# Early partial sums stored straight into the result, late ones added to it by accumulating transfers

## The chip, the cores and the metric

The kernel runs on one core of one Trainium2 chip. The metric is the device time of one execution in microseconds. A profiled execution gives a trace beside it, whose span runs from the first to the last instruction.

## What is computed

An attention through 32 memories for each of 8 heads, over 8 sequences of 576 tokens, followed by a two-layer network with a squared ReLU on all 4608 tokens. Cut to what matters here:

```
a   = softmax(phi)                          # over the 32 memories
k_m = einsum('bhsm,bhsd->bhmd', a, k);  v_m = einsum('bhsm,bhsd->bhmd', a, v)
x   = softmax(q @ k_m.T / 8) @ v_m          # heads side by side: 4608 x 512
h   = relu(x @ w_in)                        # 4608 x 2048
out = (h * h) @ w_out                       # 4608 x 512, float32
```

The kernel keeps the result transposed, as `outT` (512 x 4608) in HBM.

## The kernel before

A float32 product is made of three TensorE products of rounded halves (`x_hi`, `x_lo` and likewise for the weights). The first two sequences (`FUSED = 2`) go through both layers at once. For the other six (3456 tokens) the first layer writes its output to HBM (`r_f32`), and `second_layer` (from L1231) runs at the end, when everything else is done.

`second_layer` goes through a list of items (L1235 to L1237). An item is a stretch of tokens and `p`, one of eight pairs of blocks of 128 rows of `w_out`. Six stretches of 512 tokens are done by `products` (L1339), with a scheme that makes seven products out of eight; the 384 tokens that are left (`rest`) are done by `plain` (L1322), with ordinary products. These 384 tokens stand in the list twice: with `p` from 0 to 5 (`EARLY = 6`) ahead of all the stretches, and with `p` 6 and 7, the last quarter, behind all of them. So each of the four blocks of 128 output rows (`e` from 0 to 3, `NET = 4`) has two partial sums, some 240 us apart:

- Ahead (L1466 to L1468): when `p` is 5, ScalarE copies the four PSUM banks to SBUF rooms named `m23` and `sums`, and SyncE (SP, an engine that only issues transfers) stores them to a scratch tensor `part_f32` in HBM.
- Behind: after the last stretch SP loads the scratch tensor into the tile `part` (named `y`), L1475. Then the last `plain` items run, and `outputs` (L1407) makes five steps: VectorE adds a bank of PSUM to its part of the tile (L1412), and the sum is stored to `outT` (L1416). Block 3 goes in two halves of 192 tokens; SP issues the first four stores and ScalarE's queue the last one.

Just ahead of `outputs` on VectorE stand the sums of the last stretch (`finish_up`, L1386, whose adds and stores are recorded under L1356 and L1350).

The order on each engine is as written (a manual schedule); the tile framework sets the waits on semaphores. A transfer's semaphore is one of eight lanes, shown as `DMAHW0` to `DMAHW7`.

Of the kernel before, what the change touches and what calls it, by code (L numbers as in the profile page):

```python
# [13 lines left out]
ALU = mybir.AluOpType  # L14
# [10 lines left out]
def attn_moe_kernel(ctx: ExitStack, tc: tile.TileContext, qT, kv, phi, w_in, w_out, outT):  # L25
# [12 lines left out]
    nc = tc.nc  # L38
    ctx.enter_context(tc.manual_schedule())

    B, NQ, S = kv.shape[:3]
    P = 128
# [19 lines left out]
    FUSED = 2  # L62
# [1140 lines left out]
    for k, step in enumerate(steps):  # L1203
        i, f = step
        pieces = runs[i][0]
        n = f * P // FC
# [9 lines left out]
        g, rest = ffn1(f, parts, T, k, "act" if k in SQ_ACT else "dve", k < WHOLE and f in whole)  # L1216
# [14 lines left out]
    def second_layer():  # L1231

        late = (B - FUSED) * S
        rest = late % (2 * HALF)
# [6 lines left out]
        def load(i, room=None):  # L1241
            if i < len(items):
                t0, n, p = items[i]
                raw[i] = sp.tile([P, 4 * HALF], F32, name=room)[:, :2 * n] if room else xp.tile([P, 2 * n], F32, name="raw")
                nc.sync.dma_start(
                    out=raw[i].rearrange("p (a n) -> p a n", a=2), in_=r_f32[p][:, :, t0:t0 + n]
                )

        def square(i):
            if i < len(items):  # L1250
                n = items[i][1]
                y[i] = xp.tile([P, 2 * n if n == rest else 8 * HALF], F32, name="y", bufs=3)
                nc.scalar.activation(y[i][:, :2 * n], raw.pop(i), AF.Square)  # L1253
# [11 lines left out]
        def high(i):  # L1265
            if i < len(items):
                if items[i][1] != rest:
                    y[i] = y[i][:, HALF:]
                x[i] = [xp.tile([P, y[i].shape[-1]], F32R, name=n) for n in ("x_hi", "x_lo")]
                nc.scalar.copy(x[i][0], y[i])  # L1270
# [23 lines left out]
        def fetch_w(p):  # L1294
            if p < NFT // 2:
                w_of[p] = sp.tile([P, 2, DM], F32, name=("m01", "m45")[p % 2])
                nc.sync.dma_start(out=w_of[p], in_=w_out_f32[p])

        def weights(p):

            w = w_of.pop(p)
            half = DM // 2
            v = sp.tile([P, 4, half], F32, name=("m23", "sums")[p % 2])
            combine_w(w, v)
            W[p] = rooms_w(p) if p < 5 else [sp.tile([P, 4, half], F32R, name=f"s_{n}{p}") for n in ("hi", "lo")]
            yield
            nc.scalar.copy(W[p][0], v)
            yield
            nc.vector.tensor_tensor(out=W[p][1], in0=v, in1=W[p][0].bitcast(F32), op=ALU.subtract)

        def plain(i, acc):

            _, n, p = items[i]
            todo = [(2 * p + k, e) for k in range(2) for e in range(NET)]
            if p >= EARLY:
                todo = [(2 * p + k, e) for e in range(NET - 1) for k in range(2)]
            if p == NFT // 2 - 1:
                todo += [(f, NET - 1) for f in range(2 * EARLY, NFT)]
            for f, e in todo:
                y = x[i + f // 2 - p]  # L1320
                for j, (v, u) in enumerate(((0, 0), (1, 0), (0, 1))):
                    nc.tensor.matmul(  # L1322
                        acc[e][:, :n], wo[f][:, v, e * P:(e + 1) * P], y[u][:, f % 2 * n:(f % 2 + 1) * n],
                        start=f in (0, 2 * EARLY) and j == 0, stop=f in (2 * EARLY - 1, NFT - 1) and j == 2,
                    )

        def products(i, acc):

            p = items[i][2]
            f0, f1 = wo[2 * p], wo[2 * p + 1]  # L1330
            for m, of, col, z in (
                (0, f0, 0, 0), (1, W[p], 2, 5), (2, W[p], 1, 4), (3, W[p], 0, 3),
                (4, f1, 0, 2), (5, f1, DM // 2, 6), (6, W[p], 3, 1),
            ):
                for e in range(2):
                    for j, (v, u) in enumerate(((0, 0), (1, 0), (0, 1))):
                        at = col + e * P
                        w = of[v][:, col, e * P:(e + 1) * P] if of is W[p] else of[:, v, at:at + P]
                        nc.tensor.matmul(  # L1339
                            acc[m][:, e * HALF:(e + 1) * HALF], w, x[i][u][:, z * HALF:(z + 1) * HALF],  # L1340
                            start=p == 0 and e == 0 and j == 0, stop=p == NFT // 2 - 1 and e == 1 and j == 2,
                        )
# [43 lines left out]
        def finish_up(acc, t0):  # L1386

            m = rooms_m()
            nc.scalar.copy(m[0], acc[0])
            add(m[1], acc[1], m[0])  # L1390
            add(m[2], acc[2], m[1])
            nc.scalar.copy(m[3], acc[3])
            yield
            add(m[1], m[1], m[3])
            add(m[4], acc[4], m[0])
            store(t0, 0, 1, m[4])
            add(m[3], m[3], m[2])
            store(t0, 1, 0, m[3])
            add(m[5], acc[5], m[2])
            store(t0, 1, 1, m[5])  # L1400
            add(m[6], acc[6], m[1])
            store(t0, 0, 0, m[6])

        part_f32 = dram.tile([P, NET, rest], F32, name="part_f32")
        part = end = None

        def outputs(acc):  # L1407

            cols = [(e, 0, rest) for e in range(NET - 1)]
            cols += [(NET - 1, 0, rest // 2), (NET - 1, rest // 2, rest)]  # L1410
            for e, c0, c1 in cols:
                nc.vector.tensor_tensor(  # L1412
                    out=part[:, e, c0:c1], in0=acc[e][:, c0:c1], in1=part[:, e, c0:c1], op=ALU.add
                )
                nc_q = nc.scalar if c0 else nc.sync
                nc_q.dma_start(  # L1416
                    out=outT[e * P:(e + 1) * P, FUSED * S + c0:FUSED * S + c1], in_=part[:, e, c0:c1]
                )

        load(4, "s_hi6")  # L1420
# [8 lines left out]
        for i, (t0, n, p) in enumerate(items):  # L1429
            first, last = p == 0, p == NFT // 2 - 1  # L1430
            if n == rest:
                if p in (0, EARLY):
                    names = ("b0", "b1", "b2", "b3") if first else ("b3", "b4", "b7", "b5")
                    acc = [ps.tile([P, 512], F32, name=x) for x in names]
                plain(i, acc)
            else:
                if first:
                    acc = [ps.tile([P, 512], F32, name=f"b{(4 + m) % 8}") for m in range(7)]
                products(i, acc)
            if i >= 4:  # L1440
                load(i + 4)
            high(i + 1)
            square(i + 3)
            if due:
                next(due)
            if rest_of:
                rest_of()
                rest_of = None
            for fn, k in ((low, 1), (combine, 2)) if n == rest else ((combine, 2), (low, 1)):
                fn(i + k)  # L1450
            if end:
                next(end, None)
                end = None
            new = None
            if i in PLACES:
                new = weights(PLACES[i])
                next(new)
                fetch_w(PLACES[i] + 2)
            if due:
                next(due, None)  # L1460
            due = new
            if sum_up and next(sum_up, True):
                sum_up = None
            if n == rest and p == EARLY - 1:
                o = [sp.tile([P, 2, 2 * HALF], F32, name=x) for x in ("m23", "sums")]
                for e in range(NET):  # L1466
                    nc.scalar.copy(o[e // 2][:, e % 2, :n], acc[e][:, :n])
                    nc.sync.dma_start(out=part_f32[:, e], in_=o[e // 2][:, e % 2, :n])  # L1468
            elif last and n == rest:
                outputs(acc)  # L1470
            elif last and t0 + n == late:
                end = finish_up(acc, t0)
                next(end)
                part = xp.tile([P, NET, rest], F32, name="y", bufs=3)
                nc.sync.dma_start(out=part, in_=part_f32)  # L1475
            elif last:
                rest_of, sum_up = take_apart(acc, t0)

# [101 lines left out]
```

## Time and profile before

| | |
|---|---|
| time, median of 3 runs | 693.61 us (693.13 to 695.61) |
| the profiled execution's own time | 693.01 us |
| its span | 690.9 us |
| TensorE busy with products | 680.3 us (98%) |
| VectorE / ScalarE / GpSimd (POOL) busy | 75% / 58% / 9% |
| granted TensorE clock over the span | 0.999 of full speed |

TensorE is busy nearly all the time, so what another engine does counts only where TensorE waits for it, or after TensorE's last product. In the page's names, PE is TensorE, DVE is VectorE, ACT is ScalarE, POOL is GpSimd, SPq and ACTq are the queues of SyncE and ScalarE that issue transfers. A transfer's row has the duration of its issue; its landing is counted from the start of that issue.

### The profile page before, as it was taken

Reading aid. Unit: us, or ns where it says so; the run is one execution under the profiler, and the core shown is the slowest. Engines: PE = TensorE matmul, PEld = TensorE weight load, DVE = VectorE, ACT = ScalarE, POOL = GpSimd, SP = SyncE. Lnnn points to the kernel's source line nnn. Section 1 sums busy time; section 2 is a strip of 40 time slices with the busy share of each in tenths; the row PEclk is TensorE's granted clock in tenths of the full one; section 3 lists DMA queues with packets and bytes.
Section 4 is the critical chain, followed back from the end, with each engine's and each line's share of the span. In section 5 each row is a group of like instructions: output and inputs, shape, how many; then the busy total and the mean of one; then the engine's idle time right before and its main releaser. Section 6 shows DMA issues by size and latency. Waiting matters only on the chain.

```text
span 690.9 us, 14437 instructions
## 1 busy us (share of the span) xinstructions
PE 680.3 (98%) x5860; PEld 614.1 (89%) x5860; DVE 517.6 (75%) x888; ACT 401.6 (58%) x620; POOL 60.9 (9%) x86
## 2 busy tenths in 40 slices
PE   9899999999999999999999999999999999999998
PEld 5477798988889878888888899999999999999997
DVE  4978787987666847585847635998979798897964
ACT  2647887975554555555555565766555555555541
POOL 1322102101321010101000000000000000000000
PEclk9999999999999999999999999999999999999999
DMA  9993528263693969595946579643444536344434
GB/s 302 391 345 111 216 88 261 65 226 118 205 353 129 298 212 327 194 329 189 347 154 215 190 239 330 200 120 93 152 124 122 153 93 183 100 146 128 130 95 153
DMA packets 95218, 135.16 MB, mean 196 GB/s; under 512 B 5616, under 2 KB 60144, under 8 KB 94512
## 3 DMA queue, kind: packets, MB, share of 16 engines
q1 hardware_dynamic: 92192, 129.09, 57.0%
q10 hardware_dynamic: 2960, 5.15, 2.1%
q8 instruction: 46, 0.75, 0.5%
q14 instruction: 20, 0.16, 0.1%
HBM read 87.29 MB, written 46.92 MB: 194 GB/s over the span
## 4 chain that ended last, share of the span: by engine, by line
PE 82%; DMA 9%; ACT 5%; DVE 2%; SPq 1%; issue 1%; POOL 0%; ACTq 0%; DVEq 0%
PE b L1339 35%; PE hh L1500 13%; PE acc L748 11%; PE h L697 7%; DMA r_f<-o 7%; PE b L1322 5%; PE ps_m L430 4%; PE acc L740 3%; ACT o L1531 2%; PE h L310 2%; DMA wo<-in_w_in 1%; DMA u_hi<-in_kv 1%; ACT u_hi L577 1%; PE h L168 1%; ACT e_sb L266 1%; PE h L430 1%
## 5 line engine op out<-in xcount | busy, mean ns | idle before, releaser
L1270 ACT CAST x_hi<-y 128x1792 fp32r<-128x1792 f32 (+1 forms) x56 | 87.9, 1570 | 104.2 <-PE b L1339 50.5
L1274 DVE TENSOR_TENSOR x_lo<-y,x_hi 128x1792 fp32r<-128x1792 f32 (+1 forms) x56 | 104.7, 1870 | 44.7 <-ACT x_hi L1270 44.7
L1531 ACT ACTIVATE o<-hh 128x576 f32<-128x576 f32 x94 | 61.2, 657 | 83.4 <-PE hh L1500 52.2
L1339 PE MATMUL b<-x_hi,wo 128*128 128x256 f32 x576 | 107.8, 283 | 0.0
L1339 PEld LDWEIGHTS b<-x_hi,wo 128*128 128x128 f32 x576 | 89.9, 192 | 0.0
L1339 PE MATMUL b<-x_lo,wo 128*128 128x256 f32 x288 | 81.4, 283 | 0.0
L1263 DVE TENSOR_TENSOR y<-y 128x512 f32<-128x512 f32 x144 | 73.6, 512 | 3.3
L1339 PE MATMUL b<-x_lo,u_hi 128*128 128x256 f32 x240 | 67.5, 281 | 0.0
L1339 PE MATMUL b<-x_hi,u_hi 128*128 128x256 f32 x240 | 67.4, 281 | 0.0
L1339 PE MATMUL b<-x_hi,u_lo 128*128 128x256 f32 x240 | 67.4, 281 | 0.0
L1253 ACT ACTIVATE y<-raw 128x1024 f32<-128x1024 f32 (+1 forms) x52 | 53.6, 1031 | 4.7 <-DMA raw<-r_f 4.7
L1339 PEld LDWEIGHTS b<-x_lo,wo 128*128 128x128 f32 x288 | 55.3, 192 | 0.0
L1339 PEld LDWEIGHTS b<-x_hi,u_hi 128*128 128x128 f32 x240 | 46.0, 192 | 0.0
L1339 PEld LDWEIGHTS b<-x_lo,u_hi 128*128 128x128 f32 x240 | 45.1, 188 | 0.0
L1339 PEld LDWEIGHTS b<-x_hi,u_lo 128*128 128x128 f32 x240 | 45.0, 188 | 0.0
L748 PE MATMUL acc<-g_hi,wo 128*128 128x320 f32 (+1 forms) x256 | 43.2, 301 | 0.0
L1339 PE MATMUL b<-x_lo,s_hi 128*128 128x256 f32 x144 | 40.5, 282 | 0.0
L1339 PE MATMUL b<-x_hi,s_hi 128*128 128x256 f32 x144 | 40.5, 281 | 0.0
L1339 PE MATMUL b<-x_hi,s_lo 128*128 128x256 f32 x144 | 40.5, 281 | 0.0
L705 ACT ACTIVATE r_room<-h 128x320 f32<-128x320 f32 (+2 forms) x56 | 24.7, 442 | 26.7 <-PE h L697 25.9
L748 PEld LDWEIGHTS acc<-g_hi,wo 128*128 128x128 f32 x256 | 38.0, 188 | 0.8 <-ACT wo L677 0.8
L740 PE MATMUL acc<-g_hi,wo 128*128 128x256 f32 (+1 forms) x128 | 34.1, 409 | 0.0
(269 smaller groups left out, 1633.6 us busy)
## 6 DMA issues: line engine op xcount, KB each, us to landing
r_f<-o SPq DMA_DIRECT2D x48, 576.0 KB, 4.3
raw<-r_f SPq DMA_DIRECT2D x46, 512.0 KB, 4.0
wo<-in_w_in SPq DMA_DIRECT2D x16, 512.0 KB, 8.2
wo<-in_w_out SPq DMA_DIRECT2D x16, 512.0 KB, 7.0
kvb<-in_kv SPq DMA_DIRECT2D x28, 256.0 KB, 6.1
q_sb<-in_q SPq DMA_DIRECT2D x24, 288.0 KB, 5.3
out_t<-m SPq DMA_DIRECT2D x24, 256.0 KB, 2.3
e_sb<-in_phi SPq DMA_DIRECT2D x8, 512.0 KB, 4.2
```

Source lines behind the costliest of these rows:

```text
L430: nc.tensor.matmul(out[half][M * pr:M * (pr + 1), :y.shape[-1]], mem[hs, x, pr], y, start=True, stop=True)
L697: nc.tensor.matmul(h[:, at:at + n], u[:, qd, fs], x[:, qd], start=(i == 0), stop=(i == len(todo) - 1))
L740: nc.tensor.matmul(acc[e][:, :T], wo[f][:, e * P:(e + 1) * P], g_hi, start=first, stop=last)
L748: nc.tensor.matmul(acc[e][:, :T], wo[f][:, w, e * P:(e + 1) * P], x, start=first and x is g_hi and w == 0, stop=last and x is g_lo,)
L1253: nc.scalar.activation(y[i][:, :2 * n], raw.pop(i), AF.Square)
L1263: nc.vector.tensor_tensor(out=out, in0=in0, in1=in1, op=ALU.subtract)
L1270: nc.scalar.copy(x[i][0], y[i])
L1274: nc.vector.tensor_tensor(out=x[i][1], in0=y.pop(i), in1=x[i][0].bitcast(F32), op=ALU.subtract)
L1322: nc.tensor.matmul(acc[e][:, :n], wo[f][:, v, e * P:(e + 1) * P], y[u][:, f % 2 * n:(f % 2 + 1) * n], start=f in (0, 2 * EARLY) and j == 0 ...
L1339: nc.tensor.matmul(acc[m][:, e * HALF:(e + 1) * HALF], w, x[i][u][:, z * HALF:(z + 1) * HALF], start=p == 0 and e == 0 and j == 0, stop=p ...
L1500: nc.tensor.matmul(banks[t][:, :T], u[:, qd, fs], x[:, qd], start=(i == 0), stop=(i == len(todo) - 1))
L1531: nc.scalar.activation(r.rearrange("p (t x) -> p t x", t=NT), h[:, :, :S // NT], AF.Relu)
```

## The change

The early partial sums are stored into `outT` itself in place of the scratch tensor, by the same four transfers from SP. The load of the scratch tensor is gone. At the end VectorE no longer adds; it copies the late partial sums from PSUM to the tile, and five transfers that GpSimd issues add them to what stands in `outT` (`accum_op=ALU.add`). No transfer of `outputs` is left on SP or on ScalarE's queue.

```
-                nc.vector.tensor_tensor(
-                    out=part[:, e, c0:c1], in0=acc[e][:, c0:c1], in1=part[:, e, c0:c1], op=ALU.add
-                )
-                nc_q = nc.scalar if c0 else nc.sync
-                nc_q.dma_start(
-                    out=outT[e * P:(e + 1) * P, FUSED * S + c0:FUSED * S + c1], in_=part[:, e, c0:c1]
+                nc.vector.tensor_copy(part[:, e, c0:c1], acc[e][:, c0:c1])
+                nc.gpsimd.dma_start(
+                    out=outT[e * P:(e + 1) * P, FUSED * S + c0:FUSED * S + c1], in_=part[:, e, c0:c1], accum_op=ALU.add
                 )
...
-                    nc.sync.dma_start(out=part_f32[:, e], in_=o[e // 2][:, e % 2, :n])
+                    nc.sync.dma_start(out=outT[e * P:(e + 1) * P, FUSED * S:FUSED * S + rest], in_=o[e // 2][:, e % 2, :n])
...
-                nc.sync.dma_start(out=part, in_=part_f32)
```

On VectorE, at the end of its program, stands in a row before and after (`b3`, `b4`, `b7` and `b5` are banks of PSUM):

```order
-L1412 TENSOR_TENSOR y_8179<-b3_8181,y_8179 128x384 [waits DMAHW5_49,PE_49]
-L1412 TENSOR_TENSOR y_8179<-b4_8182,y_8179 128x384 [waits PE_49]
-L1412 TENSOR_TENSOR y_8179<-b7_8183,y_8179 128x384 [waits PE_49]
-L1412 TENSOR_TENSOR y_8179<-b5_8184,y_8179 128x192 [waits PE_49]
-L1412 TENSOR_TENSOR y_8179<-b5_8184,y_8179 128x192
+L1412 COPY y_8179<-b3_8180 128x384 [waits PE_49]
+L1412 COPY y_8179<-b4_8181 128x384 [waits PE_49]
+L1412 COPY y_8179<-b7_8182 128x384 [waits PE_49]
+L1412 COPY y_8179<-b5_8183 128x192 [waits PE_49]
+L1412 COPY y_8179<-b5_8183 128x192
```

The five adds have become five copies of the same shapes, without the wait for the load.

On GpSimd, at the end of its program:

```order
 L496 TENSOR_TENSOR a_lo2_4705<-at_4702,a_hi2_4704 128x576 [waits PE_49,Activation_49]
 L496 TENSOR_TENSOR g_room_4809<-at_4806,r_room_4808 128x576 [waits PE_49,Activation_49]
-L1576 UNCONDITIONAL_BRANCH
-L1576 ISA [waits barrier_Pool_Activation_PE_DVE_SP_gather]
+L1413 DMA out_t<-y_8179 128x384 [waits DMAHW7_49,DVE_49]
+L1413 DMA out_t<-y_8179 128x384 [waits DMAHW0_49,DVE_49]
+L1413 DMA out_t<-y_8179 128x384 [waits DMAHW1_49,DVE_49]
+L1413 DMA out_t<-y_8179 128x192 [waits DMAHW2_49,DVE_49]
+L1413 DMA out_t<-y_8179 128x192 [waits DVE_49]
+L1572 UNCONDITIONAL_BRANCH
+L1572 ISA [waits barrier_Pool_Activation_PE_DVE_SP_gather]
```

All five transfers now stand one behind another on one engine, each waiting for its copy on VectorE and (the lanes 7, 0, 1, 2) for the early store of the same output rows.

On SP, at the end of its program, this stood before (`m45`, `m23` and `m6` are the sums of the last stretch):

```order
321 L1475 DMA y_8179<-part_f32_5219 128x1536 [waits DMAHW5_49,DVE_49]
322 L1350 DMA out_t<-m45_8173 128x2x256 [waits DMAHW6_49,DVE_49]
323 L1350 DMA out_t<-m23_8172 128x2x256 [waits DVE_49]
324 L1350 DMA out_t<-m45_8173 128x2x256 [waits DMAHW0_49,DVE_49]
325 L1350 DMA out_t<-m6_8174 128x2x256 [waits DVE_49]
326 L1416 DMA out_t<-y_8179 128x384 [waits DMAHW5_49,DMAHW2_49,DVE_49]
327 L1416 DMA out_t<-y_8179 128x384 [waits DMAHW3_49,DVE_49]
328 L1416 DMA out_t<-y_8179 128x384 [waits DMAHW4_49,DVE_49]
329 L1416 DMA out_t<-y_8179 128x192 [waits DVE_49]
```

After the change the load (321) and the stores of the tile (326 to 329) are gone, and the four stores of the last stretch end SP's row of transfers.

## Rows read from the trace of the kernel before

**Rows 1.** The page: span, and busy time of each engine.

```profile
span 690.9 us, 14437 instructions
PE 680.3 (98%) x5860; PEld 614.1 (89%) x5860; DVE 517.6 (75%) x888; ACT 401.6 (58%) x620; POOL 60.9 (9%) x86
```

**Rows 2.** The chain that ended last, 660 us to the end (start us, us, what).

```profile
659.93 19.35 PE b L1339 x163
679.28 8.34 PE b L1322 x48
687.62 0.02 issue
687.65 0.36 DVE y L1412
```

**Rows 3.** Timeline of DVE, the end (start us, us, line, operation, idle before).

```profile
683.39 0.68 DVE L1356 TENSOR_TENSOR m<-b,m 128x512 f32<-128x512 f32 x1
683.99 1.10 DVE L1412 TENSOR_TENSOR y<-b,y 128x384 f32<-128x384 f32 x2
685.56 0.56 DVE L1412 TENSOR_TENSOR y<-b,y 128x384 f32<-128x384 f32 x1 [0.48 <-PE b L1322]
687.65 0.62 DVE L1412 TENSOR_TENSOR y<-b,y 128x192 f32<-128x192 f32 x2 [1.53 <-PE b L1322]
```

**Rows 4.** Timeline of the queues of SP and ACT, the end.

```profile
673.04 0.34 SPq L1475 DMA_DIRECT2D y<-part_f  x1
682.30 2.17 SPq L1350 DMA_DIRECT2D out_t<-m  x4
684.57 3.79 SPq L1416 DMA_DIRECT2D out_t<-y  x4
688.30 0.34 ACTq L1416 DMA_DIRECT2D out_t<-y  x1
```

**Rows 5.** Transfers, 640 us to the end: issuer, count, KB each, median us to landing.

```profile
y<-part_f SPq DMA_DIRECT2D x1, 768.0 KB, 4.2
out_t<-y SPq DMA_DIRECT2D x3, 192.0 KB, 2.7
out_t<-y ACTq DMA_DIRECT2D x1, 96.0 KB, 1.7
```

**Rows 6.** Queue instructions of the program's last line (ns min/median/max, first and last start).

```profile
L1576 SPq EVENT_SEMAPHORE  x8: 17/28/28, 688.4 to 690.8; - x8
L1576 SPq DRAIN  x3: 7/7/7, 690.1 to 690.4; - x3
```

**Rows 7.** POOL by form: line, operation, count | busy us, mean ns | idle before.

```profile
L725 POOL TENSOR_TENSOR g_lo<-g_room,g_hi 128x320 fp32r<-128x320 f32 x12 | 11.9, 992 | 34.1 <-ACT g_hi L721 18.1 <-DVE g_room L711 7.4 <-PE h L697 6.5
...
L620 POOL TENSOR_TENSOR w<-tmp,low 128x512 int32<-128x512 int32 x5 | 6.4, 1278 | 28.4 <-DVE tmp L613 23.4 <-ACT low L603 3.4 <-ACT g_hi L709 1.6
```

**Rows 8.** POOL's timeline from 380 us to the end.

```profile
384.93 1.57 POOL L496 TENSOR_TENSOR g_room<-at,r_room 128x576 fp32r<-128x576 f32 x1 [6.16 <-ACT r_room L495]
```

**Rows 9.** DVE by form: adds and copies from PSUM.

```profile
L1366 DVE COPY m<-b 128x512 f32<-128x512 f32 x20 | 12.4, 683 | 0.0
...
L1356 DVE TENSOR_TENSOR m<-b,m 128x512 f32<-128x512 f32 x5 | 3.3, 685 | 0.1
```

**Rows 10.** Windows (start:end, length, busy by engine, clock, DMA share, GB/s).

```profile
683.00:684.00 1.00, 1.00 (x8) 1.00 (x7) 1.00 (x3) 0.00 (x0) 0.00 (x0) 1.00 0.80 264
684.00:688.00 4.00, 3.61 (x21) 3.29 (x19) 1.99 (x6) 0.00 (x0) 0.00 (x0) 1.00 1.00 344
688.00:688.50 0.50, 0.00 (x0) 0.00 (x0) 0.27 (x2) 0.00 (x0) 0.00 (x0) 1.00 0.00 0
688.50:689.00 0.50, 0.00 (x0) 0.00 (x0) 0.00 (x0) 0.00 (x0) 0.00 (x0) 1.00 0.20 65
689.00:689.50 0.50, 0.00 (x0) 0.00 (x0) 0.00 (x0) 0.00 (x0) 0.00 (x0) 1.00 0.98 315
689.50:690.90 1.40, 0.00 (x0) 0.00 (x0) 0.00 (x0) 0.00 (x0) 0.00 (x0) 0.64 0.02 5
```

**Rows 11.** The rooms of the early sums: the stores, and DVE's next writing there.

```profile
L1468 SPq DMA_DIRECT2D part_f<-m x2: 326/354/382, 440.0 to 440.5; - x2
...
L845 DVE TENSOR_TENSOR m<-m x2: 418/419/420, 448.6 to 448.9; 128x256 f32<-128x256 f32 x2
...
DMA to landing us min/median/max: 1.9/2.0/2.0
```

## The prediction

> **What bounds the kernel now.** I read the page first: TensorE has products in hand for 680.3 of 690.9 us, VectorE for 75% and POOL for 9% [rows 1]. So an edit on another engine is worth something only where TensorE waits for it, or behind TensorE's last product. The chain that ended last says which of the two this is: from 660 us to 687.62 it is TensorE alone, L1339 and then L1322, without a gap [rows 2]. Nothing that the change touches holds TensorE up there; what counts is the tail, from 687.6 us to 690.9 us, 3.3 us long.
>
> The tail is followed step by step in the timelines. VectorE adds the two halves of block 3 in 0.62 us, from 687.65 to 688.27 [rows 3]. ACT issues the last store at 688.30 in 0.34 us [rows 4], and it lands 1.7 us after that start [rows 5], at 690.0. Only then does the end of the program follow: SP's waits run from 688.4 on, its last drains stand at 690.1 to 690.4, and the span ends at 690.9 [rows 6], 0.9 us behind the landing. The sum is 0.65 + 0.03 + 1.7 + 0.9 = 3.3 us, which is the whole tail. A microsecond more on this path is a microsecond on the time. What runs on the path twice, because a queue serves one transfer after another, costs twice.
>
> **The change, part by part.**
>
> *Early stores into the result.* The same four issues by SP, now to `outT`. Nobody waits for them at 440 us: they landed after 2.0 us, by 442.5, and the next writing into their rooms is at 448.6 [rows 11]. The cost is 0 as long as they land within some 8 us.
>
> *The load that goes.* Issued at 673.04, landing after 4.2 us [rows 4, 5], at 677.2; the first add that reads it starts at 683.99 [rows 3]. It was 6.8 us early, so taking it away gives 0.
>
> *Adds that become copies.* The trace has both forms from PSUM at 512 columns: the add with one operand in PSUM takes 685 ns, the copy 683 ns [rows 9]. So the copies end where the adds ended, near 684.55, 685.1, 686.1, 688.0 and 688.27 [rows 3]. The cost and the gain are 0.
>
> *SP and ACT rid of the stores.* SP's four stores of the last stretch are issued by 684.47 [rows 4] and keep their place, since nothing of the change stood ahead of them but the load. ACT had one issue. The gain is 0 here; these issues come back on POOL.
>
> *Five accumulating transfers on POOL.* This is the term that decides. POOL has been idle since 386.5 us [rows 8], so it reaches the first one long before the copy is there, and the early stores that it also waits for landed 240 us ago. But the trace of before has not one transfer issued by POOL, so the length of an issue, c, must be bounded. From below: 0.34 us, ACT's issue of the very same half block [rows 4]. From above there is no strict row. The nearest ones on that engine are its passes over a tile of this size: 0.99 us for 128x320 and 1.28 us for 128x512 [rows 7], between which 128x384 lies at about 1.1. I take 1.1 us, nearer to POOL's own rows, since it is POOL that works here, and I give the half blocks the same, since they have as many rows (128). With c = 1.1 the issues start at 684.57, 685.67 and 686.77 and end at 687.87. The first half of block 3 is ready at 688.0, so its issue ends at 689.13. The second half, ready at 688.27, must wait for POOL and is issued by 690.23. Before, the two halves went out on two queues at once; now they stand in a row. That alone is worth 0.8 us (1.1 less the 0.3 us between the two copies).
>
> *From the end of the issue to the landing,* L. A plain store of 96 KB took 1.7 - 0.34 = 1.36 us [rows 4, 5]; that is the lower bound. The accumulating one must first fetch the old value from HBM. A fetch alone, from the load of the scratch tensor: 4.2 us landing, less 768 KB at the 344 GB/s that the engines moved [rows 5, 10] = 2.3 us, less 0.34 us of issue, leaves 1.6 us. One behind the other they make 2.9 us, the upper bound for 16 engines that are otherwise free. I take 2.6, near the upper end, since the sum can't be written before the old value is in; the 0.3 us off are the completion, which both contain.
>
> *Sum.* 690.23 + 2.6 + 0.9 = 693.7 us of span, against 690.9: +2.8 us. On the profiled execution's own time, 693.01, this gives 695.8 us; the median of the runs is 0.6 us above that execution, so the forecast goes to 693.6 + 2.8 = 696.4 us.
>
> One rule of the Trainium skill speaks for less. "DMA: Bandwidth & Descriptors", in its specifications, gives a first byte after about 1 us for transfers that GpSimd issues and about 0.6 us for those of SP and ScalarE. An estimate from that page would put only 0.4 us on the last transfer, and the time near 694. No transfer in this trace was issued by GpSimd, so nothing here bears on it; it is the case of rival 1.
>
> **The rivals.**
>
> 1. *The tail hardly notices.* If POOL issues as fast as ACT (0.34 us), it has no backlog, and the last issue ends at 688.64. With L = 1.36 to 2.6 us the span grows by 0 to 1.2 us: 693.6 to 694.8 us. For it speaks that POOL does nothing else; against it, that no POOL pass over such a tile was anywhere near 0.34 us.
>
> 2. *POOL's issues are dearer than its passes over a tile.* The five stand in a row from 684.57 on, so from c = 1.2 on every 0.1 us more counts nearly five times. The span is 684.57 + 5c + 2.6 + 0.9. It is 3.47 us longer (0.5% of the time) from c = 1.26 on; at c = 1.5 it is 695.6, or +4.7: 698.3 us; at c = 2.0 it is +7.2: 700.8 us. A first issue that takes a microsecond or more longer than the others, by an engine that did nothing for 300 us, does the same. For it speaks that 1.26 lies only 0.16 above my value, and that POOL's passes over 128x512 took 1.28 us [rows 7]; against it, that an issue need not touch the data. This is the rival on the other side.
>
> 3. *The engines that move the data become the bound.* From 683.2 to 688 us they were full: 0.264 + 4 x 0.344 = 1.64 MB went at 344 GB/s [rows 10], the four stores of the last stretch (1.05 MB) and three of the tile (0.59 MB). If an accumulating transfer takes f times the engine time of a store, the work ends at 683.2 + (1.05 + 0.79 f) / 0.344 = 686.3 + 2.3 f. Data that ended at 689.5 had landed at 690.0, so 0.5 + 0.9 us follow: 692.3 at f = 2, before the 693.7 of my sum, so it would not show. It passes the 0.5% from f = 3 on; at f = 4 the span is 696.9, +6.0: 699.6 us. For it speaks that each row is now read twice and written once; against it, that this makes f = 2, not 4. The Trainium skill's "Collectives: The Full Stack", in the section on the bandwidth ceiling, has a reduction in the transfer engines at about half the rate of a copy because of its second read. By that f would be 2 and this rival would not come about; no run here shows it.
>
> A gain is hard to find: the tail has no step that gets shorter, since the copy takes as long as the add [rows 9] and the load was early. That the change does not do what it says is excluded by the order of instructions: the transfers are on POOL, and nothing of `outputs` is left on SP or ACT.
>
> **How the numbers follow.** I give my sum, with anything between +1.2 and +3.4 us, 0.48; rival 1 0.09, of which 0.02 for a time more than 0.5% below before; rival 2 0.25; rival 3 0.18. About 0.5% (3.5 us) is what a measurement of this kernel can tell from no change; my sum, at +2.8 us or 0.4%, stays inside. So: faster 0.02, same 0.55, slower 0.43. The range reaches from 694.0 us, inside rival 1, to 700.5 us, which holds rival 2 to c = 1.95 and rival 3 to just beyond f = 4; about 1 in 10 is left out at the top and 1 in 12 at the bottom. The likeliest case's own range is 694.8 to 697.0 us.
>
> **What would show it.** TensorE's last product should end within 0.3 us of 687.6 as before, and the five copies should take 0.55 and 0.35 us. If POOL's queue shows five transfers with starts 1.1 us apart and the last one issued near 690.2, the issue term is right; starts 0.4 us apart mean rival 1, 1.3 us and more rival 2. If the last landing comes 2.6 us behind the last issue, L is right; much more, with the windows showing the transfer engines full beyond 690 us, is rival 3. What would make all of it wrong is a difference outside the tail: TensorE waiting anywhere before 687 us, or a landing-to-end part that is no longer 0.9 us.

## The result, and the profile after

| | before | after |
|---|---|---|
| time, median of 8 runs | 693.53 us | 696.58 us (696.05 to 698.42) |
| ratio to before | | 1.0057, 95% interval 1.0045 to 1.0069 |
| second comparison, on another occasion | 693.11 us | 696.39 us, ratio 1.0045 (1.0030 to 1.0060) |
| the profiled execution's own time, and span | 693.01, 690.9 us | 697.25, 695.3 us |

The change costs 3.1 us by the medians of the first comparison and 3.3 us by those of the second, at the very line of 0.5%: one ratio lies a little over it, one a little under. The forecast was 696.4 us, +2.8.

First, the page of after (span, busy time of the engines):

```profile
span 695.3 us, 14437 instructions
PE 680.8 (98%) x5860; PEld 613.8 (88%) x5860; DVE 517.5 (74%) x888; ACT 401.8 (58%) x620; POOL 65.2 (9%) x91
```

TensorE's work is the same as in [rows 1]. In this execution its last product ends 1.1 us later than in the profiled one of before, with the same instructions; such a difference comes and goes between executions (in the runs below it ended anywhere from 685.9 to 690.3 us), so I compare the **tail**: from the start of VectorE's step on the first half of block 3, where TensorE's last product has just ended, to the end of the span. Before it was 690.9 - 687.65 = 3.2 us [rows 1, 3]. The chain that ended last in after, 660 us to the end (start us, us, what):

```profile
680.42 8.34 PE b L1322 x48
688.77 0.02 issue
688.79 0.36 DVE y L1412
689.15 0.28 DVEq L1572
689.42 0.02 issue
689.44 0.86 POOL out_t L1413
690.31 0.89 POOLq L1572
```

The tail is 695.3 - 688.79 = 6.5 us. TensorE's stretch is as without a gap as in [rows 2]; behind it the chain now goes through VectorE's copy, then through POOL. The timelines of VectorE and POOL, from 680 us:

```profile
685.13 1.09 DVE L1412 COPY y<-b 128x384 f32<-128x384 f32 x2
686.71 0.56 DVE L1412 COPY y<-b 128x384 f32<-128x384 f32 x1 [0.48 <-PE b L1322]
688.79 0.62 DVE L1412 COPY y<-b 128x192 f32<-128x192 f32 x2 [1.52 <-PE b L1322]
...
686.00 2.79 POOL L1413 DMA_DIRECT2D out_t<-y  x3 [298.35 <-DVE y L1412]
689.44 1.75 POOL L1413 DMA_DIRECT2D out_t<-y  x2 [0.65 <-DVE y L1412]
```

The copies are as long as the adds of [rows 3] to within 0.01 us. POOL had been idle for 298 us. Three issues took 2.79 us, then it waited 0.65 us for block 3, and the last two took 1.75 us, to 691.19, which is 2.4 us behind TensorE's end. POOL's issues by line (ns min/median/max, first and last start), and the landings, 684 us to the end:

```profile
L1413 POOL DMA_DIRECT2D out_t<-y x5: 862/1187/1230, 686.0 to 690.0; - x5
...
q0 software_dynamic: 720, 0.79, 55.7%
q1 hardware_dynamic: 1088, 1.05, 28.1%
...
out_t<-y POOLq DMA_DIRECT2D x3, 192.0 KB, 5.2
out_t<-y POOLq DMA_DIRECT2D x2, 96.0 KB, 4.0
```

The last issue by itself with its landing, and SP's semaphore instructions of the program's last line from the last landing on, first of before, then of after:

```profile
L1413 POOL DMA_DIRECT2D out_t<-y x1: 1216/1216/1216, 690.0 to 690.0; - x1
DMA to landing us min/median/max: 4.0/4.0/4.0
...
L1576 SPq EVENT_SEMAPHORE  x4: 17/22/28, 690.0 to 690.8; - x4
...
L1572 SPq EVENT_SEMAPHORE  x10: 17/28/6065, 687.9 to 695.2; - x10
```

An issue takes 0.86 to 1.23 us. A half block lands 4.0 us after its issue began (before: 1.7 us [rows 5]); the last one landed at 694.0, 2.8 us behind the end of its issue. From there to the end of the span it is 695.3 - 694.0 = 1.3 us, where it was 0.9 us before. Before, four of SP's semaphore instructions stood from the last landing on; now there are ten. Each of GpSimd's five transfers has a semaphore of its own that SP waits for at the end. That of the last transfer comes first, and seven other waits follow it 0.06 us apart, from 694.0 to 694.4 us.

The transfer queue q0, which carries only POOL's transfers, kept the 16 engines for 55.7% of 11.3 us = 6.3 us with 0.79 MB; the 1.05 MB of SP's stores of the last stretch kept them for 3.2 us. The windows of after (start:end, length, busy by engine, clock, share of the data engines, GB/s):

```profile
687.50:688.50 1.00, 1.00 (x8) 0.93 (x6) 0.00 (x0) 0.00 (x0) 1.00 (x2) 1.00 0.97 59
688.50:690.00 1.50, 0.25 (x2) 0.00 (x0) 0.62 (x2) 0.00 (x0) 0.85 (x3) 1.00 1.12 132
690.00:691.20 1.20, 0.00 (x0) 0.00 (x0) 0.00 (x0) 0.00 (x0) 1.20 (x2) 1.00 0.97 142
691.20:693.30 2.10, 0.00 (x0) 0.00 (x0) 0.00 (x0) 0.00 (x0) 0.00 (x0) 0.88 1.15 166
693.30:695.30 2.00, 0.00 (x0) 0.00 (x0) 0.00 (x0) 0.00 (x0) 0.00 (x0) 0.50 0.04 5
```

Before, the data engines ran empty at 688.0 and waited for the last stores [rows 10]. Now their packets fill the time until 693.3 us, at 59 GB/s in the first microsecond and at 130 to 170 behind it, where stores went at 344. So two things end near each other: POOL's row of issues with the delay behind the last one, and the work of the data engines. Which of them sets the end can't be read from this trace alone. The expectations below call the first theory QUEUE and the second ENGINES.

### The profile page after: what moved, and what is told of

Its sections match the earlier page's. It is cut to its first block, busy times and chain, and to the rows that moved or that the text cites. A ratio compares the mean times of both kernels' runs of the same rounds, so it can differ in the third digit from the quotient of the medians.

```text
span 695.3 us, 14437 instructions
## 1 busy us (share of the span) xinstructions
PE 680.8 (98%) x5860; PEld 613.8 (88%) x5860; DVE 517.5 (74%) x888; ACT 401.8 (58%) x620; POOL 65.2 (9%) x91
## 4 chain that ended last, share of the span: by engine, by line
PE 84%; DMA 8%; ACT 4%; DVE 2%; issue 0%; POOL 0%; SPq 0%; POOLq 0%; ACTq 0%; DVEq 0%
PE b L1339 34%; PE hh L1496 15%; PE acc L748 11%; PE h L697 7%; DMA r_f<-o 5%; PE b L1322 5%; PE ps_m L430 4%; PE acc L740 3%; PE h L310 2%; ACT o L1527 2%; DMA u_hi<-in_kv 1%; DMA wo<-in_w_in 1%; ACT u_hi L577 1%; PE h L168 1%; PE h L430 1%; ACT e_sb L266 1%
```

## The experiments

All tails in one table, each from one profiled execution; two executions each of two kernels show how much a tail scatters (6.5 and 6.4 us for the changed kernel, 5.3 and 5.8 for one kernel below), so a difference under 0.6 us between two single tails shows little.

| kernel | tail, us | ratio to before (95%) |
|---|---|---|
| before | 3.2 | |
| the change | 6.5, again 6.4 | 1.0057, again 1.0045 |
| e3: early sums through the result, rest as before | 3.2 | 1.0004 (0.9990 to 1.0017) |
| e1: POOL stores, no add | 4.4 | 1.0018 (1.0004 to 1.0032) |
| e2: block 3 in one transfer | 6.4 | 1.0053 (1.0035 to 1.0070) |
| e4: only block 3 accumulated | 5.8 | 1.0034 (1.0021 to 1.0046) |
| e5: only blocks 0 to 2 accumulated | 5.4 | 1.0041 (1.0026 to 1.0056) |
| e6: copies of blocks 0 to 2 on ScalarE | 6.5 | 1.0050 (1.0036 to 1.0064) |
| e7: blocks 0 to 2 accumulate 64 of 384 columns | 5.8 | 1.0040 (1.0026 to 1.0054) |
| e8, e11: block 3 accumulates 32 of 192 columns | 5.3, 5.8 | 1.0052 (1.0037 to 1.0067), 1.0047 (1.0035 to 1.0059) |
| e9: as e5, 64 of 384 columns | 3.5 | 1.0008 (0.9994 to 1.0022) |
| e10: as e5, stores, no add | 3.5 | 1.0003 (0.9987 to 1.0018) |

**The first half of the change alone.**

```
-                    nc.sync.dma_start(out=part_f32[:, e], in_=o[e // 2][:, e % 2, :n])
+                    nc.sync.dma_start(out=outT[e * P:(e + 1) * P, FUSED * S:FUSED * S + rest], in_=o[e // 2][:, e % 2, :n])
...
-                nc.sync.dma_start(out=part, in_=part_f32)
+                nc.sync.dma_start(out=part, in_=outT[:, FUSED * S:FUSED * S + rest].rearrange("(e p) t -> p e t", p=P))
```

> The first part of the change alone: the early partial sums are stored into the result and loaded back from there; adds on VectorE and stores by SP and ScalarE's queue as before the change. Both theories expect the tail of before, 3.2 us, and no difference to 693.3 us, since the early stores and the load were hidden by microseconds. A longer tail, or TensorE waiting near 440 us or ahead of 687 us, would put part of the loss on this half of the change.

Tail 3.2 us, ratio 1.0004. Where the early sums lie costs nothing; all of the loss is in the accumulating transfers.

**POOL as the issuer, without the add.**

```
-                    out=outT[e * P:(e + 1) * P, FUSED * S + c0:FUSED * S + c1], in_=part[:, e, c0:c1], accum_op=ALU.add
+                    out=outT[e * P:(e + 1) * P, FUSED * S + c0:FUSED * S + c1], in_=part[:, e, c0:c1]
```

> The changed kernel with one thing left out: the five transfers on GpSimd store the late partial sums and don't add, so the early sums are missing from the plain 384 tokens' result. I call the tail the stretch from the start of VectorE's step on the first half of block 3 (TensorE's last product ends there) to the end of the span: 3.2 us before, 6.5 us in the changed kernel. Theory QUEUE (GpSimd's five issues in a row, and a fixed fetch-and-add delay behind the last one): the issues stay at about 1.2 and 0.87 us each, the landing comes 1.4 us after the last issue's end in place of 3.1, and the tail is 4.8 us. Theory ENGINES (an accumulating transfer takes the data engines 2 to 3 times as long as a store, and the last one stands behind that work): also 4.8 us, but the windows show the engines idle between the transfers behind 688.5 us, where the changed kernel has them full until 693.3. If the issues get shorter too, part of their length belongs to the add. In total some 694.9 us against 696.6.

The timelines of VectorE and POOL at the end, POOL's issues by line, and queue and landings from 680 us:

```profile
685.90 0.62 DVE L1412 COPY y<-b 128x192 f32<-128x192 f32 x2 [1.53 <-PE b L1322]
...
686.56 1.07 POOL L1413 DMA_DIRECT2D out_t<-y  x2 [1.35 <-DVE y L1412]
...
L1413 POOL DMA_DIRECT2D out_t<-y x5: 539/539/689, 683.1 to 687.1; - x5
...
q0 software_dynamic: 288, 0.79, 21.7%
...
out_t<-y POOLq DMA_DIRECT2D x2, 96.0 KB, 1.9
```

The issue is half as long without the add, 0.54 us for most; the landing is 1.9 - 0.54 = 1.4 us behind it, the 1.36 us of before. The tail is 4.4 us, 0.4 less than expected, because the issues got shorter: the last one ended 1.7 us behind TensorE's end in place of 2.4. So POOL as the issuer is worth 1.2 us, and the add 2.1 of the 3.3. Of the 1.2 us, 0.4 lie behind the last landing: it came at 687.1 + 1.9 = 689.0 and the span ends at 690.3, 1.3 us later as in the changed kernel, though nothing is added. The same bytes kept the data engines for 21.7% of 10.3 us = 2.2 us: with the add they take 6.3 / 2.2 = 2.8 times as long.

**One issue less for block 3.**

```
-            cols = [(e, 0, rest) for e in range(NET - 1)]
-            cols += [(NET - 1, 0, rest // 2), (NET - 1, rest // 2, rest)]
+            cols = [(e, 0, rest) for e in range(NET)]
```

> The changed kernel with block 3 in one copy and one accumulating transfer of 384 tokens in place of two halves. The work on the data engines is the same, GpSimd has one issue less. Theory QUEUE: the copy ends 0.07 us earlier than the second half did and one issue of 1.2 us stands where two of 0.87 us stood, so the last issue ends 0.4 us earlier and the tail is 6.1 us. Theory ENGINES: the engines are full until the same moment, the tail stays at 6.4 to 6.6 us, or grows, if they run empty ahead of the whole block.

```profile
690.29 0.56 DVE L1411 COPY y<-b 128x384 f32<-128x384 f32 x1 [1.53 <-PE b L1322]
...
691.15 0.86 POOL L1412 DMA_DIRECT2D out_t<-y  x1 [0.86 <-DVE y L1411]
```

In these timelines of VectorE and POOL the last issue ends at 692.01, 1.7 us behind TensorE's end; with two halves it was 2.4 us. POOL was done 0.7 us earlier, and the tail is as long as before this edit, 6.4 us. The whole block landed 4.4 us after the start of its issue, at 695.5: 5.2 us behind TensorE's end, as the last half block did in the changed kernel. A fixed delay behind POOL's last issue doesn't give that; work left on the data engines does. A delay that grows with the size of the last transfer, which is 192 KB here, would give it as well; the runs that cut bytes, below, speak to that.

**Block 3 alone, and blocks 0 to 2 alone.** Both begin from the kernel before and give part of the blocks to POOL. The condition is `e == NET - 1` in e4 and `e < NET - 1` in e5; the early sums of those blocks go to `outT`, the others through the scratch tensor as before.

```
+                if e == NET - 1:
+                    nc.vector.tensor_copy(part[:, e, c0:c1], acc[e][:, c0:c1])
+                    nc.gpsimd.dma_start(
+                        out=outT[e * P:(e + 1) * P, FUSED * S + c0:FUSED * S + c1], in_=part[:, e, c0:c1], accum_op=ALU.add
+                    )
+                    continue
                 nc.vector.tensor_tensor(
...
```

> Only block 3 (the last two transfers) is accumulated by GpSimd; blocks 0 to 2 go as before the change (scratch tensor, add on VectorE, store by SP). GpSimd's last two issues stand where they stood in the changed kernel, since there they found GpSimd idle. Theory QUEUE: the tail stays as long as in the changed kernel, 6.3 to 6.5 us. Theory ENGINES: the engines are free when block 3 comes, the landing follows some 2 us after the last issue's end in place of 3.1, and the tail is 5.2 to 5.5 us. If the issues take 1.2 us and more here, the first ones of an idle GpSimd are the dear ones; at 0.87 us the size of the transfer decides.

> The other way round: blocks 0 to 2 are accumulated by GpSimd, block 3 goes as before the change (add on VectorE, one store by SP, one by ScalarE's queue). Nothing of GpSimd is left behind the last product. Theory QUEUE: the tail is that of before, 3.2 us, and the time 693.5 us. Theory ENGINES: the three accumulating transfers keep the data engines busy until 690 us or later, and the last two stores share them; they land late, the tail is 4 to 5 us, and the time 694.3 to 695.3 us.

e5 decides. Its timelines at the end (VectorE, POOL, SP, ACT) and the landings from 684 us:

```profile
688.93 0.62 DVE L1418 TENSOR_TENSOR y<-b,y 128x192 f32<-128x192 f32 x2 [1.53 <-PE b L1322]
...
686.13 2.79 POOL L1414 DMA_DIRECT2D out_t<-y  x3 [298.18 <-DVE y L1413]
...
689.31 0.34 SPq L1422 DMA_DIRECT2D out_t<-y  x1
...
689.58 0.34 ACTq L1422 DMA_DIRECT2D out_t<-y  x1
...
out_t<-y SPq DMA_DIRECT2D x1, 96.0 KB, 3.7
out_t<-y ACTq DMA_DIRECT2D x1, 96.0 KB, 3.6
```

POOL is done at 688.92, before VectorE begins block 3. SP and ACT issue block 3's stores as promptly as in [rows 4]. But these plain stores land after 3.6 to 3.7 us in place of 1.7 [rows 5], and the tail is 5.4 us, more than the 4 to 5 I had expected. The windows of e5 show what they share the data engines with:

```profile
689.00:690.00 1.00, 0.00 (x0) 0.00 (x0) 0.55 (x2) 0.00 (x0) 0.00 (x0) 1.00 1.04 112
690.00:691.00 1.00, 0.00 (x0) 0.00 (x0) 0.00 (x0) 0.00 (x0) 0.00 (x0) 1.00 1.08 163
691.00:692.00 1.00, 0.00 (x0) 0.00 (x0) 0.00 (x0) 0.00 (x0) 0.00 (x0) 1.00 1.13 216
```

They stay full for two microseconds behind the last issue, at well under the rate of stores. In e4 there is nothing ahead of block 3, and POOL's two issues are the first it makes:

```profile
688.80 0.62 DVE L1413 COPY y<-b 128x192 f32<-128x192 f32 x2 [1.52 <-PE b L1322]
...
689.48 1.90 POOL L1414 DMA_DIRECT2D out_t<-y  x2 [301.87 <-DVE y L1413]
...
out_t<-y POOLq DMA_DIRECT2D x2, 96.0 KB, 3.1
```

The landing comes 3.1 us after the start of an issue (the median of two; 3.3 us for the last), in place of 4.0, and the tail is 5.8 us, between the two expectations. That the first issue of an idle POOL takes microseconds more, which rival 2 had allowed for, is not seen: two issues took 1.90 us here and 1.75 us in the changed kernel, and the first of them 1.0 us.

**Fewer bytes, the same issues.** From the changed kernel; the columns left out keep their early sums.

```
+                c1 = c0 + 64 if e < NET - 1 else c1
```

> The changed kernel with the accumulating transfers of blocks 0 to 2 cut to their first 64 of 384 columns (the other columns of these blocks keep their early sums only); copies, number of transfers and order are the same. Theory QUEUE: GpSimd issues as before, the tail stays at 6.5 us. Theory ENGINES: if bytes decide, the engines are done with these three long before block 3 comes, and the tail falls to that of block 3 alone, 5.8 us; if rows decide (128 a transfer, whatever their length), it stays near 6.4 us.

```
+                c1 = c0 + 32 if e == NET - 1 else c1
```

> The changed kernel with the two accumulating transfers of block 3 cut to 32 of their 192 columns each (the other columns keep their early sums only). Issues and their order are the same. Theory QUEUE: the tail stays at 6.3 to 6.5 us, since a fixed delay follows the last issue. Theory ENGINES: block 3's rows go through as soon as those of blocks 0 to 2 are through, 0.7 to 1.0 us earlier than in the changed kernel: a tail of 5.5 to 5.8 us.

With the blocks ahead cut (e7), POOL's issues stand as before, 2.79 us for three and 1.75 us for two, and the tail falls to 5.8 us, that of block 3 alone. The last half block landed 3.3 us after the start of its issue in place of 4.0. So their bytes had held it up, not the issues. The 0.6 to 0.7 us between the tails are just over the scatter named above, and the times don't tell the two kernels apart; e4, with nothing ahead of block 3, shows the same tail. With block 3 cut (e8) the tail was 5.3 us, but the times did not follow: 1.0052. So I ran it again beside the changed kernel:

> The same kernel as the run with block 3's accumulating transfers cut to 32 of 192 columns, beside the changed kernel itself on one chip. Its tail was 5.3 us, but its times lay 3.6 us above before, more than the tail's 2.1 us. If the tail reading holds, it is 5.3 us again, the changed kernel's is 6.5 again, and the times differ by about 1.2 us. If the tail differs from execution to execution, one of the two falls outside 0.3 us of this.

> The changed kernel once more, beside the previous one. Theory ENGINES: a tail of 6.5 us, 1.2 us longer than with block 3 cut; theory QUEUE: equal tails.

The tail was 5.8 us this time and that of the changed kernel 6.4 us; the ratios, 1.0047 and 1.0045, are the same within their intervals. The tail with small transfers is shorter both times, by 0.6 us at least, but the times can't tell half a microsecond, and a tail can be off by 0.6 us from one execution to the next. The traces show where the two runs of the small transfers differ: blocks 0 to 2 had landed 3.5 us behind TensorE's end in e8 and 4.2 us in e11. Counted from that landing to the landing of the last half block, it was 1.1 us in both runs of the changed kernel, and 0.4 and 0.3 us with the small transfers. So block 3's own bytes hold some 0.7 us of the tail.

**An earlier start.**

```
-                nc.vector.tensor_copy(part[:, e, c0:c1], acc[e][:, c0:c1])
+                copy = nc.scalar.copy if e < NET - 1 else nc.vector.tensor_copy
+                copy(part[:, e, c0:c1], acc[e][:, c0:c1])
```

> The changed kernel, with the copies of blocks 0 to 2 on ScalarE, which is idle there, so that they need not wait behind VectorE's sums of the last stretch. The first accumulating transfer can be issued some 2.6 us earlier, the second some 1.7. Theory QUEUE (GpSimd's issues of block 3 and a fixed delay behind them): these found GpSimd idle anyway, so the tail stays at 6.5 us. Theory ENGINES: the same work on the data engines begins earlier, fills the stretch in which they wait for the first accumulation's data, and ends some 0.5 to 1.5 us earlier: a tail of 5.0 to 6.0 us, but not under the 5.8 us that the accumulation of block 3 alone costs by much.

The timelines of ACT and POOL in this kernel:

```profile
685.11 0.48 ACT L1413 COPY y<-b 128x384 f32<-128x384 f32 x1 [3.41 <-PE b L1322]
...
685.92 2.91 POOL L1414 DMA_DIRECT2D out_t<-y  x3 [297.92 <-ACT y L1413]
```

The tail stayed at 6.5 us; the expectation was wrong, and so was its ground. ScalarE stood idle for 3.41 us and was released by TensorE, not by VectorE: `plain` takes blocks 0 to 2 through `p` 6 and only finishes block 0 in the item with `p` 7, so its bank is not ready before 685.1. Nothing started 2.6 us earlier: POOL's first issue began 3.4 us ahead of TensorE's end (689.28 here) in place of 2.8, and the run tells the two theories apart in nothing.

**Is it the add, or GpSimd's presence?** e5 again, with the transfers of blocks 0 to 2 cut to 64 columns (e9, the first piece of code), or whole but without the add (e10, the second).

```
+                    c1 = c0 + 64
                     nc.gpsimd.dma_start(
...
-                        out=outT[e * P:(e + 1) * P, FUSED * S + c0:FUSED * S + c1], in_=part[:, e, c0:c1], accum_op=ALU.add
+                        out=outT[e * P:(e + 1) * P, FUSED * S + c0:FUSED * S + c1], in_=part[:, e, c0:c1]
```

> Blocks 0 to 2 accumulated by GpSimd as in the run with these blocks alone, but only the first 64 of their 384 columns (the others keep their early sums); block 3 by VectorE's add, SP and ScalarE's queue as before the change. The run with whole blocks had a tail of 5.4 us. Theory ENGINES (the last stores stood behind accumulating bytes): the engines are free when block 3's stores come, and the tail falls to 3.2 to 3.6 us. Theory PRESENCE (what costs is that GpSimd issues transfers near the end at all, through its waking or the program's closing): the tail stays above 4.5 us.

> Blocks 0 to 2 stored whole by GpSimd without the add (their early sums are missing from the result), block 3 as before the change. Theory ENGINES with the add as the cause: plain bytes are through in a third of the time, the tail is 3.2 to 3.6 us, against 5.4 with the add. Theory PRESENCE: above 4.5 us, as with the add.

The landings at the end, first of e9 and then of e10:

```profile
out_t<-y POOLq DMA_DIRECT2D x3, 32.0 KB, 2.8
out_t<-y SPq DMA_DIRECT2D x1, 96.0 KB, 1.7
out_t<-y ACTq DMA_DIRECT2D x1, 96.0 KB, 1.7
```

```profile
out_t<-y POOLq DMA_DIRECT2D x3, 192.0 KB, 2.5
out_t<-y SPq DMA_DIRECT2D x1, 96.0 KB, 1.7
out_t<-y ACTq DMA_DIRECT2D x1, 96.0 KB, 1.7
```

Tails 3.5 us both, ratios 1.0008 and 1.0003, landings of 1.7 us as before the change. What delayed the plain stores in e5 by 2 us is the adding of many bytes, and not that POOL issues transfers; that is worth the last 0.3 us at most, and it lies behind the last landing (1.1 to 1.2 us to the end of the span in both, against 0.9 before). No kernel here beats the one before.

## Why the prediction was right, point by point

The time, its size and the place were right: +2.8 us forecast, +3.1 and +3.3 measured, all of it behind TensorE's last product. That it lies at 0.5% rather than within it is the 0.3 to 0.5 us that my sum fell short, and the term that was mis-sized is the last one, from the landing to the end. The steps, counted from the start of VectorE's step on block 3:

- *Early stores, the load, the copies: 0.* Shown by e3 for the stores and the load, and by the durations for the copies. TensorE's end, named as a sign to within 0.3 us, lay 1.1 us later in this execution; that sign was set too tight for what executions differ by.
- *The issue, 1.1 us each.* The five take 0.86 to 1.23 us, 1.10 on average. But one starts before its predecessor's row has ended, so that the starts stand 0.5 to 0.9 us apart and not 1.1, and there was no backlog when block 3 came: POOL had waited 0.65 us for it. Against that stands 0.3 us which I had not counted, from the end of VectorE's copy (689.15) to the start of POOL's issue (689.44). SP in e5 started 0.02 us after the end of its add. The last issue ended 2.4 us behind TensorE's end; my sum had 690.23 - 687.65 = 2.6. That POOL's passes over a tile gave the right length is luck: without the add an issue takes 0.54 us (e1).
- *From the issue's end to the landing, 2.6 us, with 2.9 as the upper bound.* The last issue took 1.2 us, and its transfer landed 4.0 us after its start: 2.8 us (2.7 when the kernel ran again), inside the bounds. But I had built it as a fetch and a store one behind the other on engines that are otherwise free, and they were not free. With few or no bytes ahead of it the last half block took 3.3 - 1.2 = 2.1 us (e4, and e7 with the same five issues); the other 0.6 to 0.7 us is the rest of the accumulating work of blocks 0 to 2, which the sum did not have. That the size was right nevertheless is luck.
- *From the landing to the end, 0.9 us.* This is the mis-sized term: it measured 1.3 us. I took it over from the kernel before, though the prediction named it as a stretch whose change would make the sum wrong. It goes with GpSimd's transfers and not with the add: 0.9 us with none (before, e3), 1.1 to 1.2 with two to four (e4, e5, e9, e10, e2), 1.3 with five (after, e1, e6, e7, e8). Six more of SP's closing waits stand behind the last landing than before; at 0.06 us each they make nearly all of the 0.4 us.
- *Rival 1* fell. Its issues would have taken 0.34 us. Even without the add they took 0.54 us and the tail grew by 1.2 us (e1): 0.5 us is the later start of the last issue, 0.2 its later landing (1.9 us after that start against 1.7), 0.4 the longer end. The prediction's estimate of 0.4 us, from the first byte that the Trainium skill's "DMA: Bandwidth & Descriptors" gives in its specifications, was too low for the tail as well; no run here shows a first byte.
- *Rival 2* did not come about: the durations stayed under 1.26 us, and no first issue was dear.
- *Rival 3* is where I was wrong in substance. I took an accumulating transfer for f = 2 stores, because its rows are read twice and written once, and concluded that it would not show. It measured f = 2.8, by the time of the packets. In the trace three quarters of its packets of 1536 bytes took 140 ns, 2.1 times the 66 ns of a store's, but a tenth took 290 ns and more, and the mean was 195 ns; why these are slow stays open. My own formula, 686.3 + 2.3 f, moved by the 1.1 us that this execution ran late, then gives 693.8 us for the end of the data, and the windows have them end between 693.3 and 693.6. The issues and L of my sum, moved likewise, put the last landing at 692.8 + 1.1 = 693.9 us, and the data some 0.5 us ahead of it, at 693.4; the two paths end within half a microsecond of each other. Engines that are full beyond 690 us were the sign that the prediction had named for this rival. e5, with the issue path taken away, still loses 2.2 us by itself. The Trainium skill's "Collectives: The Full Stack", in the section on the bandwidth ceiling, has the reduction of a ring of cores at about half the rate of a copy, because of its second read; the rate here was 1 / 2.8 of a store's, for rows of 1536 and 768 bytes in HBM, so that half does not carry over.

So the time was right for a mixed reason, and in part by luck. Along the path of my sum the 3.3 us are 1.4 us of issues (the last one ends at 2.4 us in place of 1.0), 1.5 us of landing (2.8 in place of 1.3) and 0.4 us of the end; the sum had 1.6, 1.2 and 0. The order of POOL's issues explains part of the loss (e1: 1.2 us; the 0.7 us that e2 saves there buys nothing), and the data engines' work another. Since they run side by side, their single losses, 2.2 us in e5 and 2.6 us in e4, don't add up to the 3.3 us of both.

## What to carry to other kernels

An add that costs its engine no time is not worth moving into the transfers: VectorE's add from PSUM took as long as the copy that replaced it. At the end of a program what counts is the last transfer's issue, its landing and whatever else the data engines still have to do; accumulating transfers that are issued a few microseconds earlier delay even plain stores behind them, and transfers on a further queue can lengthen the program's end by the waits for them (0.4 us here). And where a sum names one path, price the second one to the same accuracy when it ends within a microsecond of the first.

## What the runs showed of the hardware that I had not expected

- An accumulating transfer into HBM kept the data engines 2.8 times as long as a plain store of the same bytes (6.3 against 2.2 us for 0.79 MB).
- GpSimd's issue of a store of 128 rows took 0.54 us (the first one 0.69); with the add 0.86 to 1.23 us. With the add such issues overlap by some 0.3 us: three of them took 2.79 us.
- GpSimd started its issue 0.3 us after the end of the copy that it waited for, in the changed kernel as in e1 and e4; SP started 0.02 us after (e5).
- With five transfers on GpSimd's queue, with the add or without, the span ended 1.3 us behind the last landing, with none 0.9 us: SP waits for each one's semaphore at the end, and its waits stand 0.06 us apart.
